# A seven-product block algorithm in the first layer of the second MLP, for the last 2048 of 3072 tokens

## The chip, the core and the metric

The kernel runs on one core of a Trainium2 chip. The metric is the device time of one execution in microseconds (us). TensorE multiplies matrices and writes its results to PSUM; VectorE and ScalarE do the elementwise work; GpSimd hardly takes part; SyncE issues the transfers between HBM and on-chip memory. In the rows of the profile PE is TensorE's multiplications, PEld its weight loads, DVE is VectorE, ACT is ScalarE, SPq is SyncE's queue.

## The reference

Chunked attention with a few memory keys gives 3072 tokens of 512 values; two MLPs follow, each 512 to 2048 to 512. The change touches the second one alone:

```python
def _moe2_ref(x, w_in, w_out, s, b):      # x (3072, 512), w_in (512, 2048), w_out (2048, 512)
    h = x @ w_in
    r = np.maximum(h, 0.0)
    g = s * (r * r) + b
    return (g @ w_out).astype(np.float32)
```

## The kernel before

All matrix products of the two MLPs are done in three multiplications instead of one: each operand is kept as a high and a low part whose sum is the fp32 value, and `mm3` (lines 289 to 293) adds high times high, high times low and low times high into the same PSUM tile. The three lines 291, 292 and 293 are the rows of every such product in the profile; the names on both sides of the arrow (`psH<-xh,w`, `acc<-w,gh`) tell first layer from second.

Tokens are taken in tiles of 384, eight per MLP, and the 2048 hidden values in sixteen chunks `c` of 128. One slot is one pair (tile, chunk). In a slot of the second MLP, `h2` (line 376) multiplies the four 128 by 128 blocks of the first weight with the token tile: 12 multiplications that each stream 384 token columns past loaded weights, into one of two `psH` tiles. Then the elementwise chain makes `g`: ReLU out of PSUM (line 379), square (380), scale and shift (382 or 384), high part (164), low part (168). `g` has one buffer, its two parts have three. Two slots later `out2` (line 387) uses the three blocks of 128 tokens of `g` as loaded weights and streams 512 columns of the second weight: 9 multiplications, into accumulators that fill the other half of PSUM over all sixteen chunks. `put_out` (line 327) copies a finished accumulator to SBUF, on ScalarE and VectorE in turn, into `big` tiles (four buffers), and SyncE writes them out.

The order on TensorE is that of the loop at line 551: first layer of slot n, second layer of slot n - 2, and so on without a gap. A scheduler then fills the other engines, so work whose inputs are there can be moved ahead of its place in the code. The weights of the second MLP arrive as integers of 64 bits and are unpacked on ScalarE and VectorE (`split_w`, lines 114 to 137), during the last tile of the first MLP and the first slots of the second. The tokens of a tile are loaded from HBM (`load_y`) and split into parts (`split_y`) while the tile before is computed. The first tile of an MLP is worked on in two halves of chunks, with the second tile between them.

```python
289      def mm3(o, a, b, sa, sb, first, last):
291          nc.tensor.matmul(o, sa(a[0]), sb(b[0]), start=first, stop=False)
292          nc.tensor.matmul(o, sa(a[0]), sb(b[1]), start=False, stop=False)
293          nc.tensor.matmul(o, sa(a[1]), sb(b[0]), start=False, stop=last)
```

Of the kernel before, what the change touches and what calls it, by code (L numbers as in the profile page):

```python
# [20 lines left out]
P = 128  # L21
# [28 lines left out]
def tile_attention_then_two_mlps(ctx, tc, q_in, k_in, v_in, w1, w2, s_in, b_in, out):  # L50
# [12 lines left out]

    nc = tc.nc
# [15 lines left out]
    N2 = 384  # L80
    NTILE2 = NT // N2

# [5 lines left out]
    gp = ctx.enter_context(tc.tile_pool(name="gp", bufs=3))  # L88
# [6 lines left out]
    part_dram = [dp.tile([P, KT, MAXN], F32, name="part1"), dp.tile([P, N2 // P, DM], F32, name="part2")]  # L95
# [10 lines left out]
    W = {}  # L106
# [7 lines left out]
    def split_w(c, i, raw):  # L114
# [21 lines left out]
        W[nm, c] = (hi, lo)  # L136
# [9 lines left out]
    op = [actx.enter_context(tc.tile_pool(name="op", bufs=4))]  # L146
# [116 lines left out]
    def to_x(u, ps, behind=None):  # L263
# [7 lines left out]
        for i in ins if behind else ():  # L271
            tc.add_manual_dep(i.ins, behind.ins.name,
                              mybir.DependencyInfo(mybir.DependencyClass.Sync, mybir.DependencyReason.DATA))
# [15 lines left out]
    def mm3(o, a, b, sa, sb, first, last):  # L289
# [3 lines left out]
        nc.tensor.matmul(o, sa(a[1]), sb(b[0]), start=False, stop=last)  # L293
# [10 lines left out]
    def split_g(g, n):  # L304
        gh = gp.tile([P, MAXN], F32R, tag="gh", name="gh")
        gl = gp.tile([P, MAXN], F32R, tag="gl", name="gl")
        hi_copy("gh", gh[:, :n], g[:, :n])
        sub(gl[:, :n], g[:, :n], gh[:, :n])
        return gh, gl
# [54 lines left out]

    def load_y(t):
        ys = p2["ys"].tile([P, KT, N2], F32, tag="ys", name="ys")
        nc.sync.dma_start(out=ys, in_=y_dram[:, :, t * N2:(t + 1) * N2])
# [3 lines left out]
    def split_y(t, m):  # L371
        ys, yh, yl = Y[t]
        hi_copy("yh", yh[:, m, :N2], ys[:, m, :])
        sub(yl[:, m, :N2], ys[:, m, :], yh[:, m, :N2])

    def h2(t, c):
        ps = h_mm(t, c, N2, Y[t][1:])
        g = one.tile([P, N2], F32, tag="g", name="g")
        nc.scalar.activation(out=g, in_=ps[:, :N2], func=AF.Relu)  # L379
# [5 lines left out]
        G[2, t, c] = split_g(g, N2)  # L385

    def out2(t, c):
        first, last = first_last(2, t, c)
        if first:
            accumulators(t, N2 // P)  # L390
        g = G.pop((2, t, c))
        for m in range(N2 // P):
            mm3(ACC[t][m], g, W["o", c], lambda a: a[:, m * P:(m + 1) * P], lambda a: a, first, last)
        put_out(2, t, c, DM, lambda m: out[t * N2 + m * P:t * N2 + (m + 1) * P, :])
# [87 lines left out]
    def mlp1_step(t, c):  # L482
# [41 lines left out]
    def mlp2_step(t, c):  # L524
# [91 lines left out]
```

## Time and profile before

| | us |
|---|---|
| median of 3 runs (1162.07 to 1163.25) | 1162.56 |
| the profiled execution's own time | 1160.43 |
| its span, first to last instruction | 1158.7 |
| TensorE multiplications busy, of the span | 1141.1 |
| TensorE weight loads busy | 1071.9 |
| VectorE busy | 688.4 |
| ScalarE busy | 455.2 |

The busy time of multiplications overlaps itself: each one's recorded duration reaches into the next one's, so the time of one in a stream is read from the distance between two starts. The same holds for weight loads. In rows grouped by line the columns are: line, engine, operation, output and inputs, shapes and count; then busy time in us and mean duration in ns; then the idle time before, with what ended it. In the rows in order of time, the first number is the start and the second the duration, both in us. In the rows by stretch, each engine has its busy time and in brackets its count of instructions; then come the granted clock of TensorE (1.00 is full), the share of the DMA engines and GB/s.

### The profile page before, as it was taken

The page shows a single profiled execution, that of the slowest core. Times are in us where ns is not written, and L with a number is a line of the kernel's source. Part 1 is how long each engine was busy: PE and PEld are TensorE (multiplying, and loading weights), DVE is VectorE, ACT ScalarE, POOL GpSimd, SP SyncE. Part 2 cuts the span into 40 slices and gives each one's busy share as a digit, 9 for nine tenths or more (in the row PEclk, how much of TensorE's full clock was granted, in tenths as well). Part 3 has the DMA queues.
Part 4 walks back from the last instruction along what each step waited for, and adds up shares of the span by engine and source line. Part 5 has one row for each costly group of instructions (what it writes and reads, how often), then busy time and mean ns, then how long its engine had stood idle before and what let it go on. Part 6 is the DMA issues. An engine that isn't in the chain of part 4 may idle for free.

```text
span 1158.7 us, 21163 instructions
## 1 busy us (share of the span) xinstructions
PE 1141.1 (98%) x8878; PEld 1071.9 (93%) x8878; DVE 688.4 (59%) x1430; ACT 455.2 (39%) x885; POOL 0.7 (0%) x6
## 2 busy tenths in 40 slices
PE   7989999999999999999999999999999999999998
PEld 6889999999999999999998999999999999999997
DVE  6999567776677766766799423343434344343433
ACT  4898432222222222222899544422323222232222
POOL 0000000000000000000000000000000000000000
PEclk7999999999999999999999999999999999999999
DMA  8963023112131121201874000210101000000000
GB/s 311 381 237 120 1 101 120 47 46 74 53 112 48 46 74 49 91 2 29 286 252 151 28 1 28 65 45 1 55 1 55 1 28 28 1 28 1 28 1 27
DMA packets 34271, 88.39 MB, mean 76 GB/s; under 512 B 3712, under 2 KB 12928, under 8 KB 34176
## 3 DMA queue, kind: packets, MB, share of 16 engines
q1 hardware_dynamic: 34176, 87.05, 21.6%
q8 instruction: 69, 1.13, 0.4%
q14 instruction: 26, 0.21, 0.1%
HBM read 72.88 MB, written 14.16 MB: 75 GB/s over the span
## 4 chain that ended last, share of the span: by engine, by line
PE 89%; ACT 6%; DVE 3%; issue 1%; DMA 0%; ACTq 0%
PE psH L291 14%; PE psH L293 14%; PE psH L292 14%; PE acc L292 14%; PE acc L293 14%; PE acc L291 14%; ACT raw L120 1%; PE psVS L259 1%; ACT w L134 1%; ACT raw L121 1%; PE psVS L200 1%; PE psV L259 1%; ACT g L315 1%; ACT g L316 1%; ACT gh L164 1%
## 5 line engine op out<-in xcount | busy, mean ns | idle before, releaser
L291 PE MATMUL psH<-xh,w 128*128 128x384 f32 x1024 | 346.7, 339 | 4.4 <-DVE g L317 2.4
L293 PE MATMUL psH<-xh,w 128*128 128x384 f32 x1024 | 344.7, 337 | 0.0
L292 PE MATMUL psH<-xl,w 128*128 128x384 f32 x1024 | 343.7, 336 | 0.2 <-DVE xl L168 0.2
L291 PEld LDWEIGHTS psH<-xh,w 128*128 128x128 f32 x1024 | 192.7, 188 | 13.9 <-DVE g L317 4.2
L380 DVE TENSOR_TENSOR g<-g 128x384 f32<-128x384 f32 x128 | 71.4, 558 | 219.4 <-ACT g L379 219.4
L292 PEld LDWEIGHTS psH<-xl,w 128*128 128x128 f32 x1024 | 192.7, 188 | 6.0 <-DVE xl L168 0.4
L168 DVE TENSOR_TENSOR gl<-g,gh 128x384 fp32r<-128x384 f32 x256 | 142.4, 556 | 91.3 <-ACT gh L164 88.7
L293 PEld LDWEIGHTS psH<-xh,w 128*128 128x128 f32 x1024 | 192.5, 188 | 0.2
L291 PE MATMUL acc<-gh,w 128*128 128x384 f32 x512 | 172.3, 337 | 0.0
L293 PE MATMUL acc<-gh,w 128*128 128x384 f32 x512 | 171.1, 334 | 0.0
L292 PE MATMUL acc<-gl,w 128*128 128x384 f32 x512 | 171.1, 334 | 0.0
L315 ACT ACTIVATE g<-psH 128x384 f32<-128x384 f32 x128 | 62.8, 491 | 272.8 <-PE psH L293 202.3
L379 ACT ACTIVATE g<-psH 128x384 f32<-128x384 f32 x128 | 63.1, 493 | 230.7 <-PE psH L293 227.4
L293 PE MATMUL acc<-w,gl 128*128 128x512 f32 x384 | 151.9, 396 | 0.0
L292 PE MATMUL acc<-w,gh 128*128 128x512 f32 x384 | 151.7, 395 | 0.0
L291 PE MATMUL acc<-w,gh 128*128 128x512 f32 x384 | 149.5, 389 | 1.4 <-DVE big L344 1.4
L164 ACT ACTIVATE gh<-g 128x384 fp32r<-128x384 f32 x176 | 92.5, 525 | 113.8 <-DVE g L384 99.1
L317 DVE SCALAR_TENSOR_TENSOR g<-g,psH 128x384 f32<-128x384 f32 x128 | 70.5, 551 | 99.5 <-ACT g L316 98.5
L291 PEld LDWEIGHTS acc<-gh,w 128*128 128x128 f32 x512 | 96.1, 188 | 0.8
L292 PEld LDWEIGHTS acc<-gl,w 128*128 128x128 f32 x512 | 96.1, 188 | 0.0
L293 PEld LDWEIGHTS acc<-gh,w 128*128 128x128 f32 x512 | 96.1, 188 | 0.0
L239 DVE STREAM_TRANSPOSE pt<-sm 32x128 f32<-32x128 f32 x288 | 87.2, 303 | 5.1
(62 smaller groups left out, 961.4 us busy)
## 6 DMA issues: line engine op xcount, KB each, us to landing
raw<-w SPq DMA_DIRECT2D x64, 512.0 KB, 5.1
kb<-k SPq DMA_DIRECT2D x24, 512.0 KB, 5.5
v<-v SPq DMA_DIRECT2D x24, 512.0 KB, 3.9
q<-q SPq DMA_DIRECT2D x24, 256.0 KB, 5.3
y_dram<-big SPq DMA_DIRECT2D x32, 192.0 KB, 1.9
ys<-y_dram SPq DMA_DIRECT2D x8, 768.0 KB, 4.9
out<-big SPq DMA_DIRECT2D x24, 256.0 KB, 2.1
part<-big SPq DMA_DIRECT2D x4, 192.0 KB, 3.3
```

The costliest lines, as they stand in the source:

```text
L120: nc.scalar.activation(out=f(high), in_=f(high), func=AF.Copy, scale=2.0 ** -112)
L164: return nc.scalar.activation(out=hi, in_=src, func=AF.Copy)
L168: return nc.vector.tensor_tensor(out=lo, in0=src, in1=f(hi), op=ALU.subtract)
L239: nc.vector.transpose(out=pt[k * CH:(k + 1) * CH, :, rows], in_=sm[rows, :, z, n0:n0 + CH])
L259: nc.tensor.matmul(ps[r % 2 * D:(r % 2 + 1) * D, z, o:o + CH], v[rows, (r * NC + c) * D:(r * NC + c + 1) * D], pt[rows, r, cs], start=True ...
L291: nc.tensor.matmul(o, sa(a[0]), sb(b[0]), start=first, stop=False)
L292: nc.tensor.matmul(o, sa(a[0]), sb(b[1]), start=False, stop=False)
L293: nc.tensor.matmul(o, sa(a[1]), sb(b[0]), start=False, stop=last)
L315: nc.scalar.activation(out=g[:, :n], in_=ps[:, :n], func=AF.Relu, scale=-1.0)
L317: nc.vector.scalar_tensor_tensor(out=g[:, :n], in0=g[:, :n], scalar=-1.0, in1=ps[:, :n], op0=ALU.add, op1=ALU.max)
L379: nc.scalar.activation(out=g, in_=ps[:, :N2], func=AF.Relu)
L380: nc.vector.tensor_tensor(out=g, in0=g, in1=g, op=ALU.mult)
```

## The change

Tiles of the second MLP become 384, 384 and 256 tokens, then four of 512. The first three are computed as before. For the tiles of 512, `h2` gives way to `h2_pair`, which handles two chunks at once. The first weight of two chunks is seen as two by two blocks (two halves of the 512 inputs, two chunks), the token tile as two by two blocks (two halves of the inputs, two halves of 256 tokens), and the four result blocks come from seven block products in place of eight, in Winograd's form of Strassen's algorithm. Each block product is two 128-deep steps in three parts, so six multiplications of 256 columns: 42 for a pair of chunks. The second layer of a pair is 24 multiplications of 512 columns.

The sums that go into the products are made elsewhere. Four sums of weight blocks per pair of chunks are made once (`make_s`), split into high and low parts, written to HBM, and read back for each pair of each tile (`load_s`) into places of the first weight that the products don't read. Four sums of token blocks are made per tile (`sums_y`, `split_blocks`). Seven additions per pair put the results together out of PSUM (`add` in `h2_pair`); they wait for the last multiplication into the PSUM bank that they read. The `g` chain then works on both chunks at once (`g2_pair`). The parts of `g` get four buffers in place of three, the `big` tiles three in place of four.

```diff
-    N2 = 384
-    NTILE2 = NT // N2
+    sizes2 = [384, 384, 256] + [512] * 4
+    assert sum(sizes2) == NT
+    starts2 = [sum(sizes2[:i]) for i in range(len(sizes2))]
+    NTILE2, NORM2 = len(sizes2), 3
...
-    gp = ctx.enter_context(tc.tile_pool(name="gp", bufs=3))
+    gp = ctx.enter_context(tc.tile_pool(name="gp", bufs=4))
...
+    s_dram = dp.tile([NF // 2, 4, P, 2, 2 * P], F32, name="s_dram")
...
-    op = [actx.enter_context(tc.tile_pool(name="op", bufs=4))]
+    op = [actx.enter_context(tc.tile_pool(name="op", bufs=3))]
...
+    HN = 256
+    def make_s(i):
+        a = []
+        for c in (2 * i, 2 * i + 1):
+            hi, lo = W["i", c]
+            t = wst.tile([P, DM], F32, tag="t", name="t")
+            nc.vector.tensor_tensor(out=t, in0=f(hi), in1=f(lo), op=ALU.add)
+            a.append(t)
+        (a11, a12), (a21, a22) = ((t[:, :2 * P], t[:, 2 * P:]) for t in a)
+        u = p2["ts"].tile([P, 4, 2 * P], F32, tag="ts", name="sf")
+        for j, (x, y, op) in enumerate(((a21, a22, ALU.add), (u[:, 0], a11, ALU.subtract),
+                                        (a11, a21, ALU.subtract), (a12, u[:, 1], ALU.subtract))):
+            nc.vector.tensor_tensor(out=u[:, j], in0=x, in1=y, op=op)
+            sp = p2["s"].tile([P, 2, 2 * P], F32R, tag="s", name="s")
+            nc.scalar.activation(out=sp[:, 0], in_=u[:, j], func=AF.Copy)
+            sub(sp[:, 1], u[:, j], sp[:, 0])
+            nc.sync.dma_start(out=s_dram[i, j], in_=f(sp))
+    SW, pairs = {}, [(t, i) for t in range(NORM2, NTILE2) for i in range(NF // 2)]
+    def load_s(n):
+        if n < len(pairs):
+            for j in range(4):
+                SW[n, j] = WT["i", 2 * ((4 * n + j) % 8) + 1][:, :, :2 * P]
+                nc.sync.dma_start(out=f(SW[n, j]), in_=s_dram[pairs[n][1], j])
+    def sums_y(t):
+        ys = load_tokens(t)
+        (b11, b12), (b21, b22) = ((ys[:, k:k + 2, :HN], ys[:, k:k + 2, HN:]) for k in (0, 2))
+        ts = p2["ts"].tile([P, 2, 2, HN], F32, tag="ts", name="ts")
+        t2, t3 = ts[:, 0], ts[:, 1]
+        for o, x, y in ((t3, b22, b12), (b12, b12, b11), (t2, b22, b12)):
+            nc.vector.tensor_tensor(out=o, in0=x, in1=y, op=ALU.subtract)
+        Y[t] = [b11, b21, t2, t3, b12, b22, t2], []
+    def split_blocks(t, j):
+        src, parts = Y[t]
+        if j < 6:
+            if j % 3 == 0:
+                p2["xt"] = [xp.tile([P, 3, 512], F32R, tag=f"{nm}{j // 3 ^ 1}", name=nm) for nm in ("xh", "xl")]
+        else:
+            p2["xt"] = [p2["ts"].tile([P, 1, 512], F32R, tag=f"{nm}2", name=nm) for nm in ("xh", "xl")]
+            nc.vector.tensor_tensor(out=src[6], in0=src[1], in1=src[2], op=ALU.subtract)
+        xh, xl = (x[:, j % 3, :].rearrange("p (k n) -> p k n", k=2) for x in p2["xt"])
+        hi_copy("yh", xh, src[j])
+        sub(xl, src[j], xh)
+        parts.append((xh, xl))
+    def h2_pair(n):
+        t, i = pairs[n]
+        blocks = Y[t][1]
+        wa, wb = W["i", 2 * i], W["i", 2 * i + 1]
+        lo_k, hi_k = (lambda w: tuple(x[:, :2 * P] for x in w)), (lambda w: tuple(x[:, 2 * P:] for x in w))
+        s1, s2, s3, s4 = ((SW[n, j][:, 0], SW[n, j][:, 1]) for j in range(4))
+        big = ps_a.tile([P, 2, 512], F32, tag="a", name="psG")
+        hs = [ps_h.tile([P, 512], F32, tag="h", name="psG") for _ in range(2)]
+        place = [big[:, 0, :HN], big[:, 0, HN:2 * HN], big[:, 1, :HN], big[:, 1, HN:2 * HN],
+                 hs[0][:, :HN], hs[0][:, HN:2 * HN], hs[1][:, :HN]]
+        last = []
+        for o, a, b in zip(place, (lo_k(wa), hi_k(wa), s2, s3, s1, s4, hi_k(wb)), blocks):
+            for k in range(2):
+                mm = mm3(o, a, b, lambda x: x[:, k * P:(k + 1) * P], lambda x: x[:, k, :], k == 0, k == 1)
+            last.append(mm)
+        q1, q2, q6, q7, q5, q3, q4 = place
+        hb = p2["ts"].tile([P, 2, 512], F32, tag="hb", name="hb")
+        m1, u2, u3 = (wst.tile([P, DM], F32, tag="t", name=nm)[:, :HN] for nm in ("m1", "u2", "u3"))
+        def add(o, x, q, behind):
+            wait(nc.vector.tensor_tensor(out=o, in0=x, in1=q, op=ALU.add), last[behind])
+        wait(nc.scalar.activation(out=m1, in_=q1, func=AF.Copy), last[1])
+        add(hb[:, 0, :HN], m1, q2, 1)
+        add(u2, m1, q6, 3)
+        add(u3, u2, q7, 3)
+        add(u2, u2, q5, 5)
+        add(hb[:, 1, HN:], u3, q5, 5)
+        add(hb[:, 0, HN:], u2, q3, 5)
+        add(hb[:, 1, :HN], u3, q4, 6)
+        return hb
+    def g2_pair(t, i, hb):
+        nc.vector.scalar_tensor_tensor(out=hb, in0=hb, scalar=0.0, in1=hb, op0=ALU.max, op1=ALU.mult)
+        nc.scalar.activation(out=hb, in_=hb, func=AF.Identity, scale=s_sb, bias=b_sb)
+        for z in range(2):
+            G[2, t, 2 * i + z] = split_g(hb[:, z], 512)
...
-            op.append(ctx.enter_context(tc.tile_pool(name="op2", bufs=4)))
-            p2["ys"] = ctx.enter_context(tc.tile_pool(name="ysp", bufs=1))
+            op.append(ctx.enter_context(tc.tile_pool(name="op2", bufs=3)))
+            p2["ys"] = p2["ts"] = ctx.enter_context(tc.tile_pool(name="ysp", bufs=1))
+            p2["s"] = ctx.enter_context(tc.tile_pool(name="sp", bufs=2))
...
+        if hf + 4 <= n < hf + 4 + NF and n % 2 == 0:
+            make_s((n - hf - 4) // 2)
+        if t == 2 and c in (8, 9, 10):
+            split_blocks(NORM2, c - 8)
+        if t == 2 and c == 10:
+            load_s(0)
...
+    load_s(1)
+    for j in range(3, 7):
+        split_blocks(NORM2, j)
+    behind = [(NORM2 - 1, NF - 2), (NORM2 - 1, NF - 1)]
+    for n_, (t, i) in enumerate(pairs):
+        hb = h2_pair(n_)
+        load_s(n_ + 2)
+        if i == 3 and t + 1 < NTILE2:
+            sums_y(t + 1)
+        if i == NF // 2 - 1 and t + 1 < NTILE2:
+            for j in range(7):
+                split_blocks(t + 1, j)
+        g2_pair(t, i, hb)
+        for slot in behind:
+            out2(*slot)
+        behind = [(t, 2 * i), (t, 2 * i + 1)]
+    for slot in behind:
+        out2(*slot)```

The first order that matters is TensorE's. In the code before, a slot's 12 first-layer rows of 384 columns are followed by 9 second-layer rows of 512; here the last rows of such a slot's first layer (`w0` is the first weight, `w1` the second) and the first of the second layer:

```order
L291 MATMUL psH_10318<-xh_9625,w0_10_7668 128x384
L292 MATMUL psH_10318<-xl_9626,w0_10_7668 128x384
L293 MATMUL psH_10318<-xh_9625,w0_10_7668 128x384
L291 MATMUL acc0_10085<-w1_8_7552,gh_10271 128x512
L292 MATMUL acc0_10085<-w1_8_7552,gh_10271 128x512
L293 MATMUL acc0_10085<-w1_8_7552,gl_10272 128x512
```

After the change, the seventh product of a pair and the first rows of the second layer of the pair before (`psG` are the PSUM tiles of the products; `mm3` stands at lines 302 to 304 there):

```order
L302 MATMUL psG_9362<-xh_9169,w0_5_7245 128x256
L303 MATMUL psG_9362<-xl_9170,w0_5_7245 128x256
L304 MATMUL psG_9362<-xh_9169,w0_5_7245 128x256
L302 MATMUL psG_9362<-xh_9169,w0_5_7245 128x256
L303 MATMUL psG_9362<-xl_9170,w0_5_7245 128x256
L304 MATMUL psG_9362<-xh_9169,w0_5_7245 128x256
L302 MATMUL acc0_9334<-w1_2_7020,gh_9326 128x512
L303 MATMUL acc0_9334<-w1_2_7020,gh_9326 128x512
L304 MATMUL acc0_9334<-w1_2_7020,gl_9327 128x512
```

Rows of 256 columns stand where rows of 384 stood, 42 in a row for a pair, and 24 rows of the second layer follow; nothing else is on TensorE between them.

The second is VectorE's in the tiles of 512. Before, two slots of a late tile give:

```order
L380 TENSOR_TENSOR g_10738<-g_10738 128x384
L384 TENSOR_SCALAR g_10738<-g_10738,s_sb_90,b_sb_91 128x384
L168 TENSOR_TENSOR gl_10743<-g_10738,gh_10742 128x384
L380 TENSOR_TENSOR g_10770<-g_10770 128x384
L384 TENSOR_SCALAR g_10770<-g_10770,s_sb_90,b_sb_91 128x384
L168 TENSOR_TENSOR gl_10775<-g_10770,gh_10774 128x384
```

After, one pair of chunks gives:

```order
L478 TENSOR_TENSOR hb_9696<-m1_9697,psG_9651 128x256
L478 TENSOR_TENSOR u2_9698<-m1_9697,psG_9651 128x256
L478 TENSOR_TENSOR u3_9699<-u2_9698,psG_9651 128x256
L478 TENSOR_TENSOR u2_9698<-u2_9698,psG_9652 128x256
L478 TENSOR_TENSOR hb_9696<-u3_9699,psG_9652 128x256
L478 TENSOR_TENSOR hb_9696<-u2_9698,psG_9652 128x256
L478 TENSOR_TENSOR hb_9696<-u3_9699,psG_9653 128x256
L491 SCALAR_TENSOR_TENSOR hb_9696<-hb_9696 128x1024
L175 TENSOR_TENSOR gl_9715<-hb_9696,gh_9714 128x512
L175 TENSOR_TENSOR gl_9719<-hb_9696,gh_9718 128x512
```

Seven additions out of PSUM, one square of 1024 columns and two low parts stand where six operations of 384 columns stood; scale and shift are on ScalarE alone.

The third is VectorE's at the start of the second MLP, where the last weights are unpacked (`t`, `raw`, `w0_13`) between the `g` operations of the first slots. Before:

```order
L380 TENSOR_TENSOR g_7408<-g_7408 128x384
L128 SCALAR_TENSOR_TENSOR t_7895<-raw0_13_7244,t_7895 128x512
L125 SCALAR_TENSOR_TENSOR t_7933<-raw1_13_7246 128x512
L168 TENSOR_TENSOR w1_12_7869<-t_7857,w1_12_7869 128x512
L128 SCALAR_TENSOR_TENSOR t_7933<-raw1_13_7246,t_7933 128x512
L168 TENSOR_TENSOR gl_7413<-g_7408,gh_7412 128x384
```

After, from the low part of the same slot to that of the next:

```order
L175 TENSOR_TENSOR gl_7417<-g_7412,gh_7416 128x384
L175 TENSOR_TENSOR s_7844<-sf_7842,s_7844 128x256
L420 TENSOR_TENSOR sf_7842<-sf_7842,t_7838 128x256
L398 TENSOR_TENSOR g_7454<-g_7454 128x384
L420 TENSOR_TENSOR sf_7842<-t_7838,sf_7842 128x256
L175 TENSOR_TENSOR s_7849<-sf_7842,s_7849 128x256
L132 SCALAR_TENSOR_TENSOR t_7886<-raw1_12_7205 128x512
L132 SCALAR_TENSOR_TENSOR t_7924<-raw0_13_7248 128x512
L175 TENSOR_TENSOR gl_7459<-g_7454,gh_7458 128x384
```

The sums of `make_s` (`sf`, `s`) are scheduled from the third slot on, mixed with the rest of the unpacking, and the unpacking of the last chunks is spread over more slots.

## Rows read from the trace of the kernel before

**Rows 1.** The page: busy time by engine; granted clock in 40 slices.

```profile
PE 1141.1 (98%) x8878; PEld 1071.9 (93%) x8878; DVE 688.4 (59%) x1430; ACT 455.2 (39%) x885; POOL 0.7 (0%) x6
PEclk7999999999999999999999999999999999999999
```

**Rows 2.** What TensorE waited for in the second MLP: us, times, longest.

```profile
PE acc L291 <- DVE big L344: 1.4, 1, 1.4
```

**Rows 3.** TensorE in order of time, one slot of the second MLP.

```profile
901.07 0.39 PE L291 MATMUL acc<-w,gh 128*128 128x512 f32 x1
...
902.92 0.39 PE L293 MATMUL acc<-w,gl 128*128 128x512 f32 x1
903.15 0.33 PE L291 MATMUL psH<-xh,w 128*128 128x384 f32 x1
...
905.09 0.33 PE L293 MATMUL psH<-xh,w 128*128 128x384 f32 x1
905.26 0.39 PE L291 MATMUL acc<-w,gh 128*128 128x512 f32 x1
```

**Rows 4.** The ReLU of line 379, one per slot: first and last start.

```profile
L379 ACT ACTIVATE g<-psH x108: 492/492/492, 700.3 to 1148.3; 128x384 f32<-128x384 f32 x108
```

**Rows 5.** Multiplications in order of time after attention's, in the first MLP.

```profile
269.74 0.44 PE L291 MATMUL psH<-xh,w 128*128 128x384 f32 x1
270.02 0.34 PE L292 MATMUL psH<-xl,w 128*128 128x384 f32 x1
...
270.89 0.33 PE L291 MATMUL psH<-xh,w 128*128 128x384 f32 x1
```

**Rows 6.** The weight loads of the same stretch, in order of time.

```profile
269.73 0.19 PEld L291 LDWEIGHTS psH<-xh,w 128*128 128x128 f32 x1
269.84 0.19 PEld L292 LDWEIGHTS psH<-xl,w 128*128 128x128 f32 x1
270.02 0.19 PEld L293 LDWEIGHTS psH<-xh,w 128*128 128x128 f32 x1
```

**Rows 7.** By stretch: a stretch with much DMA traffic, in the first MLP.

```profile
600.00:608.00 8.00, 8.00 (x47) 7.74 (x45) 7.97 (x15) 8.00 (x17) 0.00 (x0) 1.00 0.75 242
```

**Rows 8.** VectorE and ScalarE by line and shape, 700 to 1157 us.

```profile
L380 DVE TENSOR_TENSOR g<-g 128x384 f32<-128x384 f32 x108 | 60.3, 558 | 199.2 <-ACT g L379 199.2
...
L164 ACT ACTIVATE gh<-g 128x384 fp32r<-128x384 f32 x108 | 56.6, 524 | 99.4 <-DVE g L384 99.1
...
L382 ACT ACTIVATE g<-g,b_sb,s_sb 128x384 f32<-128x384 f32 x12 | 8.5, 706 | 6.3 <-DVE g L380 6.3
L346 ACT ACTIVATE big<-acc 128x512 f32<-128x512 f32 x14 | 8.3, 593 | 7.9 <-PE acc L293 7.8
L344 DVE COPY big<-acc 128x512 f32<-128x512 f32 x7 | 4.8, 691 | 6.7 <-ACT big L346 6.7
```

**Rows 9.** VectorE's low part of `g`, in order of time, in Rows 3's slot.

```profile
903.46 0.56 DVE L168 TENSOR_TENSOR gl<-g,gh 128x384 fp32r<-128x384 f32 x1 [0.59 <-ACT gh L164]
```

**Rows 10.** By stretch: six stretches of 16 us, 624 to 720, and their sum.

```profile
624.00:640.00 16.00, 15.50 (x76) 13.71 (x77) 15.86 (x29) 13.52 (x26) 0.00 (x0) 1.00 0.26 82
640.00:656.00 16.00, 16.00 (x82) 14.47 (x81) 7.87 (x14) 9.01 (x17) 0.00 (x0) 1.00 0.00 1
...
sum 96.00, PE 95.50 PEld 86.24 DVE 43.46 ACT 51.32 POOL 0.00; mean PE 15.92 PEld 14.37 DVE 7.24 ACT 8.55 POOL 0.00
```

**Rows 11.** The end of the span, in order of time, all engines.

```profile
1153.77 1.28 ACT L346 ACTIVATE big<-acc 128x512 f32<-128x512 f32 x2 [3.33 <-PE acc L293]
...
1154.02 0.39 PE L293 MATMUL acc<-w,gl 128*128 128x512 f32 x1
...
1154.40 0.69 DVE L344 COPY big<-acc 128x512 f32<-128x512 f32 x1 [3.37 <-ACT big L346]
```

**Rows 12.** The page's DMA issues: size and median us to landing.

```profile
out<-big SPq DMA_DIRECT2D x24, 256.0 KB, 2.1
```

More of the change, by code (lines that the diff above doesn't have):

```diff
@@ L135, in split_w @@
         sub(lo, f(t), hi)
-        W[nm, c] = (hi, lo)
+        W[nm, c], WT[nm, c] = (hi, lo), parts
         yield
@@ L292, in mm3 @@
         nc.tensor.matmul(o, sa(a[0]), sb(b[1]), start=False, stop=False)
-        nc.tensor.matmul(o, sa(a[1]), sb(b[0]), start=False, stop=last)
+        return nc.tensor.matmul(o, sa(a[1]), sb(b[0]), start=False, stop=last)
     G, ACC = {}, {}
@@ L372, in split_y @@
         ys, yh, yl = Y[t]
-        hi_copy("yh", yh[:, m, :N2], ys[:, m, :])
-        sub(yl[:, m, :N2], ys[:, m, :], yh[:, m, :N2])
+        n = sizes2[t]
+        hi_copy("yh", yh[:, m, :n], ys[:, m, :])
+        sub(yl[:, m, :n], ys[:, m, :], yh[:, m, :n])
     def h2(t, c):
-        ps = h_mm(t, c, N2, Y[t][1:])
-        g = one.tile([P, N2], F32, tag="g", name="g")
-        nc.scalar.activation(out=g, in_=ps[:, :N2], func=AF.Relu)
+        n = sizes2[t]
+        ps = h_mm(t, c, n, Y[t][1:])
+        g = one.tile([P, MAXN], F32, tag="g", name="g")[:, :n]
+        nc.scalar.activation(out=g, in_=ps[:, :n], func=AF.Relu)
         nc.vector.tensor_tensor(out=g, in0=g, in1=g, op=ALU.mult)
@@ L389, in out2 @@
         if first:
-            accumulators(t, N2 // P)
+            accumulators(t, sizes2[t] // P)
         g = G.pop((2, t, c))
-        for m in range(N2 // P):
+        for m in range(sizes2[t] // P):
             mm3(ACC[t][m], g, W["o", c], lambda a: a[:, m * P:(m + 1) * P], lambda a: a, first, last)
-        put_out(2, t, c, DM, lambda m: out[t * N2 + m * P:t * N2 + (m + 1) * P, :])
+        put_out(2, t, c, DM, lambda m: out[starts2[t] + m * P:starts2[t] + (m + 1) * P, :])
     def attn_steps():
@@ L540, in mlp2_step @@
             weights_to(w2, 52 + 4 * n, 0)
-        if nxt < NTILE2 and c0 + 2 <= c < c0 + 2 + KT:
-            split_y(nxt, c - c0 - 2)
+        if first and 2 <= c < 2 + KT:
+            split_y(1, c - 2)
+        if t == 0 and hf + 2 <= c < hf + 2 + KT:
+            split_y(2, c - hf - 2)
+        if hf + 4 <= n < hf + 4 + NF and n % 2 == 0:
[4 more added lines that the diff above has]
+            load_s(0)
         yield
@@ L548, in tile_attention_then_two_mlps @@
         order = [(0, c) for c in range(HF[mlp])] + [(1, c) for c in range(NF)] + [(0, c) for c in range(HF[mlp], NF)]
-        order += [(t, c) for t in range(2, NTILE1 if mlp == 1 else NTILE2) for c in range(NF)]
+        order += [(t, c) for t in range(2, NTILE1 if mlp == 1 else NORM2) for c in range(NF)]
         seq += [(step, out_mm, t, c) for t, c in order]
-    for n_ in range(len(seq) + 2):
-        if n_ < len(seq):
-            step, _, t, c = seq[n_]
-            parts = step(t, c)
-            next(parts)
+    for n_, (step, _, t, c) in enumerate(seq):
+        parts = step(t, c)
+        next(parts)
         if n_ >= 2:
@@ L558, in tile_attention_then_two_mlps @@
             out_mm(t, c)
-        if n_ < len(seq):
-            next(parts)
+        next(parts)
+    load_s(1)
[15 more added lines that the diff above has]
+    for slot in behind:
+        out2(*slot)
 def pack(q, k, v, mem_k, mem_v):
```

38 lines of the change are left out of this document (24 added, 14 removed).

## The prediction

> **What bounds the kernel now.** I read the page first: multiplications fill 98% of the span at full granted clock from the second slice on, VectorE 59%, ScalarE 39% [rows 1]. Then the waits of the second MLP alone: TensorE waited there for anything but itself once, 1.4 us in some 535 [rows 2]. So this stage lasts as long as its stream of multiplications, and the change is priced by how many there are and how far apart they start. One slot in order of time gives both distances: nine second-layer multiplications of 512 columns from 901.07 to 903.15, so 0.231 us each, and twelve first-layer ones of 384 from 903.15 to 905.26, so 0.176 each [rows 3]. The ReLU, one per slot, confirms the period over 107 slots: (1148.3 - 700.3) / 107 = 4.187 us [rows 4].
>
> **What goes and what comes on TensorE.** The 2304 tokens behind the first two tiles were six tiles of 384, 96 slots: 96 x 4.187 = 401.9 us go. What comes: the second layer's columns stay the same in number, 32 pairs x 24 + 16 slots x 6 = 864 multiplications of 512, at 0.231: 199.6 us. The first layer becomes 32 x 42 = 1344 multiplications of 256 columns for the products and 16 x 12 = 192 of 256 for the tile of 256 tokens: 1536 x c. Everything hangs on c, the distance between two starts at 256 columns, which the trace does not show for this kind of product. The change is even at c = (401.9 - 199.6) / 1536 = 0.1317 us, and each nanosecond is 1.54 us of time. Seven products for eight save an eighth of the columns, but a distance that shrank less than the columns would give it back.
>
> **The value of c.** Shrinking with the columns would give 0.176 x 256 / 384 = 0.117. A line through this stage's two sizes, 0.176 at 384 and 0.231 at 512, gives 0.1205. In the first MLP 384 columns take (270.89 - 270.02) / 5 = 0.174 [rows 5], and the line from there to 0.231 gives 0.117. The other limit is the weight load that each multiplication has. Its recorded 0.19 us is longer than any of these values, but it is not its distance: where TensorE comes from attention's small products, two loads start at 269.73 and 269.84, so a load occupies its path for 0.11 us, and the next waits for the multiplication [rows 6]. The first multiplication there, whose load is not hidden, is followed 0.28 us later, the second 0.17 us later [rows 5]: 0.28 = 0.11 + 0.17, a load shown and a load hidden. So the low end is 0.111 (a load and its start), the high end 0.174, no gain below 384 columns, if loads hid less well than I read. I take 0.120, the line of the same stage: gain 1536 x (0.1317 - 0.120) = 18.0 us. Loads and multiplications would then be nearly equal, 0.11 against 0.12, still with the multiplication ahead.
>
> The Trainium skill, "TensorE: Matmul & The Clock Gate", section "Back-to-back issue gap", gives N / 2.4 + 2.5 ns for a single multiplication's gap, so 109 ns at 256 columns; by it the sum would be an estimated 1536 x 0.0225 = 35 us of gain. The same formula gives 162 and 216 ns where rows 3 show 176 and 231, so the measurement decides and I keep 0.120.
>
> **Work on the other engines.** Prices of 256 and 1024 columns come from 558 ns at 384 and 691 at 512 on VectorE [rows 8]: about 0.43 and 1.22 us. In the tiles of 512 a pair lasts 24 x 0.231 + 42 x 0.12 = 10.6 us on TensorE. VectorE has 7 x 0.43 + 1.22 + 2 x 0.69 = 5.6 us per pair, and per tile some 13 more operations of 512 columns (sums, low parts, copies), 1.1 us per pair: 63%. ScalarE has less: a copy, scale and shift of 1024 columns (between 0.71 and, scaled from 384 columns, 1.9 us) and two high parts of 0.6. The chain behind the last product is 0.43 + 1.22 + 1.9 + 0.6 + 0.7 = 4.9 us to the first chunk's parts, 5.6 to the second's; they are needed after the second layer of the pair before (5.5) and the next pair's products (5.0), so 5 us are to spare. PSUM is free half a microsecond after the last product and wanted 5.5 us after it. At a tile's end seven splits of 0.69 stand on VectorE before the square, which takes most of that spare time and none of TensorE's.
>
> Each pair reads 1 MB of sums back, about 100 GB/s, with a pair's time to land; SyncE is in order, so a read that waits for its place holds up the token load and the outputs behind it, which have 5 us or more too. Traffic does not slow the stream: at 242 GB/s, 47 multiplications of 384 columns started in 8 us, 0.170 each [rows 7].
>
> The weight sums cost VectorE 2 x 0.69 + 8 x 0.43 = 4.8 us for a pair of chunks, 38 us in all. From 624 to 720 us VectorE is busy 43.5 of 96 us, so 52 are free; but the first 16 us are full, 15.9 [rows 10], and the order puts the sums right there. What they displace is the unpacking of late chunks, which nobody waits for yet. The `g` chain may slip: a low part ended at 904.02 [rows 9] and its first reader on TensorE starts two slots after the 901.07 one's followers, at 901.07 + 2 x 4.19 = 909.45, so 5.4 us to spare. In the order, the longest stretch between two low parts is 11 operations, about 6.5 us for a slot of 4.19. Between 0 (all hidden) and 8 us (the sums that the order puts into the first 32 us, 3.5 x 4.8 = 16.8, less the 8.3 that are free there by rows 10); I take 1, with the two tile transitions, since the slip of one slot is inside the spare time. Adding work excludes a gain.
>
> The end: today the last multiplication starts at 1154.02 and VectorE's last copy at 1154.40 [rows 11]. With four copies per tile and three `big` buffers, the fourth waits for the first one's output to land. The first copy can start when its pair of accumulators is done, six multiplications (1.4 us) before the stream's end; it takes 0.59 and lands 2.1 us later [rows 8, 12], 1.3 us after the end, and the fourth then takes 0.69: it ends near 2.0, where 0.7 was; 1.3 us. In the first MLP the same wait falls inside the 3 us before that accumulator is written again; 0, at worst 0.5 at each of its eight tiles.
>
> **The sum.** 18.0 - 1.0 - 1.3 = 15.7 us. The profiled execution takes 1160.43, so it would take 1144.7; the median of the runs lies 2.1 above it, so 1162.56 - 15.7 = 1146.9, rounded 1147. About 0.2% (2.3 us) is what a measurement of this kernel can tell from no change.
>
> **The rivals.** First, c near the load's own distance, 0.111 to 0.116 [rows 6]: 24 to 32 us of gain, 1133 to 1140. For it: lines from the first MLP bend that way; against: both sizes seen here lie 0.015 above their columns' pace. Second, the other side: weight loads become the bound. The mechanism is the hand-over of the loaded weights: at 384 columns a load of 0.19 has 0.17 to overlap with; if two loads cannot follow each other faster than the load's recorded time less the 0.015 by which they overlap now, c is 0.174, and the cost is 1536 x 0.042 = 65 us, 1228; halfway, 0.145, it is 20 us, 1185. It decides from 0.1317 on. For it: no full-width fp32 product of this short length is in the stage; against: the 0.11 between two starts. Third, the slipping chain: VectorE's sums in the busy first slots, or a read of sums that holds SyncE's queue, take 5 to 12 us, 1152 to 1160; it decides where a slip passes 5.4 us. Fourth, c between 0.126 and 0.131, because load and multiplication disturb each other when nearly equal: 1155 to 1165, about no change. That the products are not done as said I exclude by the order: 42 rows of 256 columns, then 24 of 512.
>
> The first rows that TensorE runs after attention show hidden loads at 0.17. The Trainium skill, same page, section "The mechanism" of its part on packing small matmuls, says that a load overlaps a running multiplication only where their row groups differ. By that rule every product would show its load, 0.11 + 0.12, and the time would be 1162.56 + 1536 x 0.098 = 1313 us; the steady 0.17 behind the first 0.28 [rows 5] speaks against it, and I give it 1 in 100, within the slower cases.
>
> **How the numbers follow.** Forecast (c 0.116 to 0.125, small waits), 1140 to 1155: 0.60. The low rival: 0.13. The slipping chain: 0.10. About even, 1160 to 1165: 0.06. Weight loads the bound: 0.11. Faster is then 0.60 + 0.13 + 0.09 = 0.82, the same 0.05, slower 0.13. The range from 1136 to 1163 leaves out half of the low rival and the slow cases, 2 in 10.
>
> **What would show it.** In the changed profile, 42 starts of 256 columns should span 5.0 us and 24 of 512 columns 5.5; loads should start 0.12 apart, right behind the multiplications' starts. A wait of TensorE on `gl`, `hb` or `w0` rows means the third rival, products 0.14 or more apart with loads back to back the second. The last copy should wait for a transfer. I am wrong if a pair takes over 11.2 us, which is what its 512 tokens take today (2.67 slots x 4.187).

## The result, and the profile after

The changed kernel takes 1149.91 us (median of 4 runs, 1149.35 to 1150.90) where the kernel before, run beside it, takes 1162.32 (1161.11 to 1163.25): a ratio of 0.9895, interval 0.9878 to 0.9912, 12.4 us less. The forecast was 15.7 us less, 1147, with a range of 1136 to 1163. Its sign held and the time lies in the range. But one term of the sum is off by some 7 us, twice as much as the whole, and another by 2.6 us the other way.

The profiled execution took 1149.35 us, its span 1147.6; that of before was 1160.43. The page, as in [rows 1]:

```profile
PE 1124.5 (98%) x9262; PEld 1057.3 (92%) x9262; DVE 767.9 (67%) x1617; ACT 475.0 (41%) x890; POOL 0.7 (0%) x6
PEclk7999999999999999999999999999999999999999
```

TensorE still fills 98% of a span that is 11.1 us shorter, with more multiplications. One pair of chunks on TensorE in order of time (start, duration, instruction), which answers to [rows 3]:

```profile
905.93 0.28 PE L302 MATMUL psG<-xh,w 128*128 128x256 f32 x1
...
910.84 0.28 PE L304 MATMUL psG<-xh,w 128*128 128x256 f32 x1
910.96 0.40 PE L302 MATMUL acc<-w,gh 128*128 128x512 f32 x1
...
912.12 0.39 PE L304 MATMUL acc<-w,gl 128*128 128x512 f32 x1
...
916.43 0.28 PE L302 MATMUL psG<-xh,w 128*128 128x256 f32 x1
```

The 42 multiplications of the seven products take 910.96 - 905.93 = 5.03 us, 0.120 each, and the 24 of the second layer 916.43 - 910.96 = 5.47: a pair in 10.50 us. That the period holds can be seen in the copy that opens each pair's additions, ScalarE's on line 480 (count, duration min/median/max, first and last start):

```profile
L480 ACT ACTIVATE m<-psG x32: 363/383/384, 806.7 to 1129.5; 128x256 f32<-128x256 f32 x32
```

(1129.5 - 806.7) / 31 = 10.41, since the first of the 31 distances holds only 12 second-layer multiplications and is 2.7 us shorter; the other 30 are 10.50. VectorE's operations by shape, the counterparts of [rows 8] (busy us and mean ns; idle before):

```profile
L491 DVE SCALAR_TENSOR_TENSOR hb<-hb 128x1024 f32<-128x1024 f32 x32 | 39.2, 1225 | 0.9
L478 DVE TENSOR_TENSOR hb<-u,psG 128x256 f32<-128x256 f32 x96 | 34.5, 416 | 0.0
```

TensorE's waits between 100 and 640 us (in all, times, longest; [rows 2] has one of 1.4 us for the second MLP, and before 600 us the kernel before has none):

```profile
PE acc L302 <- DVE big L355: 5.2, 4, 2.3
PE acc L302 <- DVE big L351: 1.5, 1, 1.5
```

From 640 us to the end the same view is empty: TensorE waits for no `gl`, `hb` or `w0`. So the second MLP goes as the forecast says, and something new happens ahead of it. Between the first second-layer multiplication of the second MLP and the last of all lie 632.23 to 1142.14 = 509.9 us, where 624.50 to 1154.02 = 529.5 lay before: 19.6 us less. The first of these starts, however, comes 7.7 us later, and behind the last one the span has 5.4 us in place of 4.6. The ledger of the two profiled executions is -19.6 + 7.7 + 0.8 = -11.1 us.

### The profile page after: what moved, and what is told of

Its sections match the earlier page's. It is cut to its first block, busy times and chain, and to the rows that moved or that the text cites. A ratio compares the mean times of both kernels' runs of the same rounds, so it can differ in the third digit from the quotient of the medians.

```text
span 1147.6 us, 22472 instructions
## 1 busy us (share of the span) xinstructions
PE 1124.5 (98%) x9262; PEld 1057.3 (92%) x9262; DVE 767.9 (67%) x1617; ACT 475.0 (41%) x890; POOL 0.7 (0%) x6
## 4 chain that ended last, share of the span: by engine, by line
PE 87%; DVE 5%; ACT 5%; DMA 2%; issue 1%; SPq 0%; DVEq 0%; ACTq 0%
PE acc L302 14%; PE acc L303 14%; PE acc L304 14%; PE psH L302 9%; PE psH L304 9%; PE psH L303 9%; PE psG L304 5%; PE psG L303 5%; PE psG L302 5%; PE psVS L266 1%; DVE pt L246 1%; PE psVS L207 1%; ACT raw L127 1%; DMA raw<-w 1%; ACT w L141 1%
## 5 line engine op out<-in xcount | busy, mean ns | idle before, releaser
L302 PE MATMUL psH<-xh,w 128*128 128x384 f32 (+1 forms) x704 | 235.4, 334 | 3.7 <-DVE g L328 2.0
L304 PE MATMUL psH<-xh,w 128*128 128x384 f32 (+1 forms) x704 | 233.8, 332 | 0.0
L303 PE MATMUL psH<-xl,w 128*128 128x384 f32 (+1 forms) x704 | 233.4, 332 | 0.2 <-DVE xl L175 0.2
L326 ACT ACTIVATE g<-psH 128x384 f32<-128x384 f32 x128 | 63.0, 492 | 278.9 <-PE psH L304 207.0
L302 PE MATMUL acc<-gh,w 128*128 128x384 f32 x512 | 173.2, 338 | 4.7 <-DVE big L355 3.2
L304 PE MATMUL acc<-gh,w 128*128 128x384 f32 x512 | 172.2, 336 | 0.0
L303 PE MATMUL acc<-gl,w 128*128 128x384 f32 x512 | 172.2, 336 | 0.0
L302 PE MATMUL acc<-w,gh 128*128 128x512 f32 x384 | 150.4, 392 | 2.0 <-DVE big L355 2.0
L303 PE MATMUL acc<-w,gh 128*128 128x512 f32 x384 | 150.6, 392 | 0.0
L304 PE MATMUL acc<-w,gl 128*128 128x512 f32 x384 | 150.1, 391 | 0.0
L302 PEld LDWEIGHTS psH<-xh,w 128*128 128x128 f32 x704 | 133.0, 189 | 8.5 <-DVE g L328 2.7
L303 PEld LDWEIGHTS psH<-xl,w 128*128 128x128 f32 x704 | 133.0, 189 | 2.4 <-DVE xl L175 0.4
L304 PEld LDWEIGHTS psH<-xh,w 128*128 128x128 f32 x704 | 133.0, 189 | 0.2
L304 PE MATMUL psG<-xh,w 128*128 128x256 f32 x448 | 126.9, 283 | 0.0
L303 PE MATMUL psG<-xl,w 128*128 128x256 f32 x448 | 126.9, 283 | 0.0
L302 PE MATMUL psG<-xh,w 128*128 128x256 f32 x448 | 126.7, 283 | 0.0
L175 DVE TENSOR_TENSOR gl<-g,gh 128x384 fp32r<-128x384 f32 (+1 forms) x176 | 95.8, 544 | 29.7 <-ACT gh L171 27.1
L302 PEld LDWEIGHTS acc<-gh,w 128*128 128x128 f32 x512 | 96.5, 189 | 6.2 <-DVE big L355 3.8
L304 PEld LDWEIGHTS acc<-gh,w 128*128 128x128 f32 x512 | 96.7, 189 | 0.0
L303 PEld LDWEIGHTS acc<-gl,w 128*128 128x128 f32 x512 | 96.7, 189 | 0.1
## 6 DMA issues: line engine op xcount, KB each, us to landing
raw<-w SPq DMA_DIRECT2D x64, 512.0 KB, 4.7
w<-s_dram SPq DMA_DIRECT2D x128, 256.0 KB, 3.6
kb<-k SPq DMA_DIRECT2D x24, 512.0 KB, 5.5
v<-v SPq DMA_DIRECT2D x24, 512.0 KB, 3.9
s_dram<-s SPq DMA_DIRECT2D x32, 256.0 KB, 2.0
q<-q SPq DMA_DIRECT2D x24, 256.0 KB, 5.4
y_dram<-big SPq DMA_DIRECT2D x32, 192.0 KB, 1.9
out<-big SPq DMA_DIRECT2D x24, 256.0 KB, 2.1
```

The costliest lines, as they stand in the source:

```text
L175: return nc.vector.tensor_tensor(out=lo, in0=src, in1=f(hi), op=ALU.subtract)
L304: return nc.tensor.matmul(o, sa(a[1]), sb(b[0]), start=False, stop=last)
L326: nc.scalar.activation(out=g[:, :n], in_=ps[:, :n], func=AF.Relu, scale=-1.0)
```

## Where the 7.7 us went

The same first-layer multiplication of the first MLP starts 0.9 us later than before at 100 us, 2.0 at 150, 4.1 at 200, and stays about there until 563 us, where 4 us come at once. The last three places are ends of tiles or of a half tile, where accumulators are copied into `big` tiles. The 0.9 us at 100 are not: 1.4 us are there at 35 us, before the first copy into a `big` tile at 73 us, and other profiled executions with three buffers, such as that of the doubled reads below, have nothing of it at 100 us. They are a difference between executions. At 563 us, VectorE's copies and TensorE in order of time (in brackets the idle time before and what ended it):

```profile
558.72 0.56 DVE L355 COPY big<-acc 128x384 f32<-128x384 f32 x1 [0.78 <-ACT big L357]
...
563.33 0.34 PE L302 MATMUL acc<-gh,w 128*128 128x384 f32 x1
565.39 0.56 DVE L355 COPY big<-acc 128x384 f32<-128x384 f32 x1 [1.71 <-DMA y_dram<-big]
566.00 0.44 PE L302 MATMUL acc<-gh,w 128*128 128x384 f32 x1 [2.34 <-DVE big L355]
...
566.88 0.52 PE L303 MATMUL acc<-gl,w 128*128 128x384 f32 x1
567.20 0.52 PE L304 MATMUL acc<-gh,w 128*128 128x384 f32 x1
...
570.08 0.37 PE L302 MATMUL acc<-gh,w 128*128 128x384 f32 x1
```

Three copies (two of them ScalarE's) are done by 559.5; the fourth has no buffer until the first output has landed, at 565.4, and TensorE needs the accumulator that it empties. The wait has a tail: behind it ten distances of 0.32 us stand (566.88 to 570.08), nearly twice the usual 0.17, 1.5 us more in all. By stretch (length, busy time and count of each engine, granted clock, DMA share, GB/s) the clock is at the lower of its two levels there, 1.2 in place of 2.4 GHz, after TensorE stood nearly idle from 563 to 566:

```profile
563.00:566.00 3.00, 0.67 (x4) 0.35 (x2) 1.29 (x4) 0.52 (x1) 0.00 (x0) 1.00 0.87 337
566.88:569.76 2.88, 2.88 (x11) 2.88 (x10) 1.11 (x2) 2.36 (x5) 0.00 (x0) 0.50 0.93 277
```
Why the output took so long is in the DMA issues from 558 to 567 us (count, KB each, median us to landing):

```profile
raw<-w SPq DMA_DIRECT2D x2, 512.0 KB, 5.7
ys<-y_dram SPq DMA_DIRECT2D x1, 768.0 KB, 6.8
y_dram<-big SPq DMA_DIRECT2D x4, 192.0 KB, 6.5
```

The first three of the four outputs stand behind a token load of 768 KB and weights of 512 KB and land after some 6.5 us; the median of all 32 on the page of the profile is 1.9. The Trainium skill, "SBUF — State Buffer", section "The DMA setup-cost knee", fits a transfer's time in us as 2 + bytes / 436,000, by which 192 KB would take an estimated 2.45. The measured median of 1.9 is near that, the 6.5 behind other transfers far from it. In the kernel before, the outputs at this place were late too, with nobody waiting for them (its issues from 552 to 562 us):

```profile
y_dram<-big SPq DMA_DIRECT2D x4, 192.0 KB, 5.4
```

At 198 us it is another chain. Token tile 0 is done in two halves, and the first half's four parts are read back into `big` tiles before the sums are formed there; with three, the fourth part is fetched only when a sum has left:

```profile
193.84 1.48 DVE L351 TENSOR_TENSOR big<-big,acc 128x384 f32<-128x384 f32 x3
194.42 1.29 SPq L358 DMA_DIRECT2D y_dram<-big  x3
196.33 0.32 SPq L345 DMA_DIRECT2D big<-part  x1
198.82 0.55 DVE L351 TENSOR_TENSOR big<-big,acc 128x384 f32<-128x384 f32 x1
199.42 0.45 PE L302 MATMUL acc<-gh,w 128*128 128x384 f32 x1 [1.50 <-DVE big L351]
```

Out, landed, in, landed: 4.4 us between the end of the first sum (194.4) and the fourth's start, more than the accumulator can wait. At 150 us, the end of tile 1, TensorE waits 0.8 us for the fourth copy. There the outputs land in 1.9 us, and the copy stands behind three of attention's transposes in VectorE's order; in the kernel before it stood ahead of them.

## The experiments

My theory: products at 0.120 are the gain, and the three `big` buffers cost what lies ahead of the second MLP. The rivals: the late start comes with the new second MLP (weight sums, transitions, reads), or the weight loads limit the products, so that a part of the gain is lost there.

**Three buffers in the kernel before.** The edit, in the kernel before, and nothing else:

```
-    op = [actx.enter_context(tc.tile_pool(name="op", bufs=4))]
+    op = [actx.enter_context(tc.tile_pool(name="op", bufs=3))]
```

> The kernel before with three big buffers in place of four up to the end of the first MLP, nothing else. Theory (the loss in the first MLP is the fourth copy of an accumulator, which waits for the first one's output to land): TensorE waits on big at ends of tiles of the first MLP, the second MLP begins some 7 to 8 us later than in the kernel before, about 1170 us. Rival (the loss comes from another part of the change, such as the order or the wider parts of g): no change, 1162 to 1163.

Measured: 1165.60 us against 1161.90, ratio 1.0031 (1.0021 to 1.0040): 3.7 us, half of what I expected. The waits at 150 and 198 us are there, with the 4 to 5 us by 250 us; the jump at 563 is not. The kernel opens a second pool, `op2`, when the last tile of the first MLP begins, and that still had four; the outputs at 563 us, of the tile before, are already copied into it.

**Both pools.** The same edit, and `bufs=4` to 3 for `op2` also.

> The kernel before with three big buffers in place of four in both pools, the one of the tiles of the first MLP and the one that takes over in its last tile. Theory, that the late start of the second MLP in the changed kernel is all due to the number of big buffers: the pool of the tiles alone gave 1165.6 with 4.5 to 5 us lost by 250 us and no jump at 563 us; with the second pool cut too the jump at about 563 us must come back, 3 to 5 us with its multiplications at the lower clock behind it, so 1169 to 1170, and the second MLP's first output multiplication starts about 8 us later than in the kernel before. Rival, that the jump belongs to the change of the second MLP itself (its transitions or its prepared sums): no jump, about 1166.

Measured: 1168.99 (1168.09 to 1170.36) against 1161.72, ratio 1.0060 (1.0043 to 1.0077): 7.3 us. TensorE's waits between 100 and 645 us:

```profile
PE acc L291 <- DVE big L344: 6.5, 4, 2.8
PE acc L291 <- DVE big L340: 1.7, 1, 1.7
```

They stand at the places of the changed kernel's, under the old line numbers, with 1.5 us more in sum, and the second MLP's first output multiplication starts at 632.11, 7.6 us later than before. No part of the new second MLP is in this kernel, so its weight sums and transitions are not needed for the late start. Each start is that of one execution: in the other runs of the changed kernel with three buffers in both pools it lies between 630.2 and 633.8 us.

**Four buffers in the changed kernel.** `op` from 3 to 4; to have room, the parts of `g` get three buffers instead of four.

```
-    gp = ctx.enter_context(tc.tile_pool(name="gp", bufs=4))
+    gp = ctx.enter_context(tc.tile_pool(name="gp", bufs=3))
-    op = [actx.enter_context(tc.tile_pool(name="op", bufs=3))]
+    op = [actx.enter_context(tc.tile_pool(name="op", bufs=4))]
```

> The changed kernel with four big buffers up to the end of the first MLP; to make room the parts of g have three buffers, not four. Theory (buffer): the second MLP begins at 623 us as in the kernel before, about 1142.5 us. Rival (loss from elsewhere): 1150. Should three buffers for g hold the pairs up, TensorE waits on gl or gh after 800 us, and a pair lasts over 10.4 us.

Measured: 1146.09 (1145.20 to 1148.54), ratio 0.9862 (0.9845 to 0.9879), 3.8 us better than the changed kernel and not the 7.4 expected, for the same reason: `op2` still had three. The waits at 150 and 198 us are gone, those from 563 us on are not. The products stay at 0.120 with three `g` buffers.

**Four in both pools.** The edit above and `op2` from 3 to 4.

> As the run with four big buffers, and four of them in the second MLP too. Theory (the last copy waits for a transfer at the end): 1.3 us less than that run, about 1141; the last copy follows the third without a wait. Rival: the end is set by the transfers themselves, no change.

Measured: 1141.49 (1140.57 to 1143.27), ratio 0.9821 (0.9807 to 0.9836). It is the fastest kernel here, 20.4 us below the kernel before and 8.4 below the change. That the expected 1141 was met is luck: from the run with four buffers in one pool it was to be 1.3 us and is 4.6, because `op2` also serves the last two ends of the first MLP, and that run had been expected 3.6 us too low. TensorE's waits between 100 and 645 us are again the single one of [rows 2], and from 552 to 562 us the outputs land as late as in the changed kernel, with nobody waiting for them:

```profile
PE acc L302 <- DVE big L355: 1.4, 1, 1.4
```

```profile
y_dram<-big SPq DMA_DIRECT2D x4, 192.0 KB, 7.0
```

The first output multiplication of the second MLP starts at 625.93 here, so 6.3 of the 7.7 us are gone. The 1.4 that are left stand beside no wait that the kernel before doesn't have.

The end of the span also shows what a fourth buffer is worth there. The last copies, of the changed kernel and of this one, in order of time:

```profile
1142.14 0.39 PE L304 MATMUL acc<-w,gl 128*128 128x512 f32 x1
1143.95 0.69 DVE L355 COPY big<-acc 128x512 f32<-128x512 f32 x1 [1.42 <-DMA out<-big]
```

```profile
1134.92 0.39 PE L304 MATMUL acc<-w,gl 128*128 128x512 f32 x1
1135.97 0.69 DVE L355 COPY big<-acc 128x512 f32<-128x512 f32 x1 [0.67 <-ACT big L357]
```

1.81 us behind the last multiplication with three, 1.05 with four: the tail's wait for a landed output is real and costs 0.8.

**Eight products, 512 columns.** The changed kernel with the first layer of its four tiles of 512 done plainly: no sums, no reads, no additions, 24 multiplications of 512 columns for a pair where seven products had 42 of 256.

```
-        for o, a, b in zip(place, (lo_k(wa), hi_k(wa), s2, s3, s1, s4, hi_k(wb)), blocks):
-            for k in range(2):
...
+        for z in range(2):
+            ps = ps_h.tile([P, 512], F32, tag="h", name="psG")
+            for k, xx in enumerate(Y[t][1]):
+                mm3(ps, W["i", 2 * i + z], xx, lambda a: a[:, k * P:(k + 1) * P], lambda a: a, k == 0, k == KT - 1)
```

> The changed kernel with the plain first layer in the tiles of 512: 24 multiplications of 512 columns per pair of chunks, no sums of weights or tokens, no reads of sums; the second layer is as in the changed kernel. Theory (TensorE's stream bounds the stage, and what the other engines do for the seven products is hidden): a pair takes 24 x 0.228 = 5.47 in place of 42 x 0.12 = 5.04 us, so 32 x 0.43 = 14 us more, about 1164. Rival (sums, additions and reads cost TensorE time in the changed kernel): the difference is smaller, 1150 to 1158.

Measured: 1159.61 (1156.89 to 1162.02), ratio 0.9977 (0.9967 to 0.9988), 9.7 us above the change. The stretch of the second MLP is 521.9 us, 12.0 more than with seven products. So of its 19.6 us, 12.0 are the seven products, and 7.6 come with the wider tiles. The medians differ by less than the stretch; in the profiled execution of this run the second MLP also starts 2.0 us earlier than in the changed kernel's. I had expected 14 for the stretch; here is why it is less. One pair of this kernel on TensorE:

```profile
902.12 0.39 PE L302 MATMUL acc<-w,gh 128*128 128x512 f32 x1
...
907.56 0.39 PE L302 MATMUL psG<-xh,w 128*128 128x512 f32 x1
...
913.00 0.39 PE L302 MATMUL acc<-w,gh 128*128 128x512 f32 x1
```

48 multiplications in 10.88 us are 0.2267 each, not the 0.231 of [rows 3]. In a stream of one width the distance is shorter. In the changed kernel's pair above, the first five behind the change of width take (912.12 - 910.96) / 5 = 0.232 and the nineteen others (916.43 - 912.12) / 19 = 0.2268. In the kernel before every run of 512 columns but one is nine long, and all nine average 0.231. The one is its last, 27 in a row up to the 1154.02 of [rows 11]:

```profile
1148.09 0.39 PE L291 MATMUL acc<-w,gh 128*128 128x512 f32 x1
...
1150.17 0.39 PE L291 MATMUL acc<-w,gh 128*128 128x512 f32 x1
```

The first nine distances take (1150.17 - 1148.09) / 9 = 0.231 there and the seventeen behind them (1154.02 - 1150.17) / 17 = 0.2265, so the shorter distance could be read before the change.

**Eight products, 256 columns.** As the last one, but in blocks of 256: 48 multiplications of 256 columns for a pair in place of 42.

> As the run with the plain first layer in tiles of 512, but each product in blocks of 256 columns: 48 multiplications of 256 per pair of chunks in place of 24 of 512. Theory (0.12 us per multiplication of 256 columns, whoever uses it, and TensorE's stream bounds the stage): 48 x 0.12 = 5.75 us per pair, 0.3 more than with 24 of 512 (5.44) and 0.72 more than with 42: some 10 us above that run, 23 above the changed kernel, about 1170 to 1173. Rival (the changed kernel's stage is bound by something besides the stream): less than 15 us above the changed kernel.

Measured: 1171.89 (1170.88 to 1172.94), ratio 1.0079 (1.0064 to 1.0094), 22.0 above the change. 32 x 6 x 0.12 = 23.0 was to come. At equal block size the eighth product costs what its multiplications say; the plain layer gets part of that back by streaming 512 columns.

**No weight sums.** `make_s` writes raw parts of the weights to where the sums belong and computes nothing, so the products are of other numbers.

```
-            nc.vector.tensor_tensor(out=u[:, j], in0=x, in1=y, op=op)
...
+            nc.sync.dma_start(out=s_dram[i, j], in_=f(WT["i", 2 * i + j // 2][:, :, j % 2 * 2 * P:(j % 2 + 1) * 2 * P]))
```

> The changed kernel without the sums of weight blocks: parts of the weights themselves are written in their place, so VectorE and ScalarE do none of that work and the products are of other numbers. Theory (the sums are hidden): 1149 to 1150, no change beyond 1 us. Rival (they hold up the g chain at the start of the second MLP, my third rival): 5 to 8 us less, 1142 to 1145.

Measured: 1149.62 (1146.78 to 1153.12), ratio 0.9886 (0.9858 to 0.9915); the difference to the change, 0.3 us, is below what can be told. By stretch of 16 us from 624 to 720 us, the sums of the changed kernel and of this one, as in [rows 10]:

```profile
sum 96.00, PE 94.00 PEld 84.91 DVE 78.81 ACT 64.30 POOL 0.00; mean PE 15.67 PEld 14.15 DVE 13.13 ACT 10.72 POOL 0.00
```

```profile
sum 96.00, PE 93.44 PEld 84.57 DVE 49.84 ACT 54.59 POOL 0.00; mean PE 15.57 PEld 14.10 DVE 8.31 ACT 9.10 POOL 0.00
```

29 us of VectorE's work vanish and TensorE is no busier. The stretch of the second MLP, 633.76 to 1143.50, is 509.7 us long, against 509.9 with the sums. The sums are hidden.

**Reads twice.** Each read of weight sums is issued twice, 2 MB per pair.

```
-                nc.sync.dma_start(out=f(SW[n, j]), in_=s_dram[pairs[n][1], j])
+                for _ in range(2):
+                    nc.sync.dma_start(out=f(SW[n, j]), in_=s_dram[pairs[n][1], j])
```

> The changed kernel with every read of weight sums done twice, so 2 MB per pair. Theory (reads are hidden and traffic does not slow the stream): 1150, products still 0.12 apart. Rival (the queue of SyncE or the traffic counts): TensorE waits on w0 tiles, over 1155.

Measured: 1148.75 (1146.65 to 1150.21), ratio 0.9879 (0.9862 to 0.9896), the same as the change. The products stay at 0.120, and TensorE waits for none of the reads; the one new wait is 0.8 us for a `big` tile at 667 us. Reads of sums have room for as much again.

**Halved products.** Each product multiplication is cut into two of 128 columns: 84 for a pair, the same columns, twice the weight loads.

```
-            for k in range(2):
-                mm = mm3(o, a, b, lambda x: x[:, k * P:(k + 1) * P], lambda x: x[:, k, :], k == 0, k == 1)
+            for m in range(2):
+                for k in range(2):
+                    mm = mm3(o[:, m * P:(m + 1) * P], a, b, lambda x: x[:, k * P:(k + 1) * P],
+                             lambda x: x[:, k, m * P:(m + 1) * P], k == 0, k == 1)
```

> The changed kernel with every multiplication of the seven products cut into two of 128 columns: 84 per pair in place of 42, each with its weight load. It asks how near 256 columns are to the point where the loads set the distance. Theory (a load occupies 0.11 us, so two multiplications cannot start closer than 0.111): 84 x 0.111 = 9.3 us per pair in place of 5.0, 32 x 4.3 = 137 us more, about 1287, and the first rival of the prediction's price for loads stands. Rival (the distance keeps shrinking with the columns, as from 512 to 384 to 256, to 0.065 at 128): 84 x 0.065 = 5.5 us, 14 us more, 1164.

Measured in a single execution: 1291.66 us, 142 above the change, near the 137 of the theory and far from the 14 of its rival. Multiplications and loads in order of time:

```profile
999.84 0.19 PEld L303 LDWEIGHTS psG<-xl,w 128*128 128x128 f32 x1
999.90 0.28 PE L303 MATMUL psG<-xl,w 128*128 128x128 f32 x1
999.95 0.19 PEld L304 LDWEIGHTS psG<-xh,w 128*128 128x128 f32 x1
1000.01 0.28 PE L304 MATMUL psG<-xh,w 128*128 128x128 f32 x1
1000.06 0.19 PEld L302 LDWEIGHTS psG<-xh,w 128*128 128x128 f32 x1
1000.12 0.28 PE L302 MATMUL psG<-xh,w 128*128 128x128 f32 x1
```

Half the columns start 0.111 us apart, not 0.06, with loads every 0.11 that overlap the multiplication before. The bound is thus 0.111, and 256 columns at 0.120 are just above it. That the load sets it, and not the multiplication, is argued: it equals the 0.11 between the two loads of [rows 6]; no run here changes the loads alone. The Trainium skill, "TensorE: Matmul & The Clock Gate", section "LDWEIGHTS (loading the stationary operand)", gives P / 1.2 ns for the P columns of a load, 107 ns for 128. The 0.111 agrees within 4%; the recorded 0.19 is not the load's share of the path.

## Why the forecast was right, and where not

**The distance c** was forecast at 0.120 from a line through 384 and 512 columns, and came out at 0.1198 over 1344 multiplications. Its low end, 0.111, read from two loads after attention, is the bound that the halved products show. The second rival, loads that cannot follow each other so fast, is refuted by them, and so is the prediction's 1313 us, for loads that would not overlap at all. The 47 multiplications in 8 us, read from [rows 7] as 0.170 each, include two that had started before; 45 start there, 0.173 apart, which bears out the same point, that the traffic does not slow them. The pair was to take 10.6 us and takes 10.50.

**The stage** was to gain 18.0 - 1.0 = 17.0 us and gained 19.6. The step that failed is "the second layer's columns stay the same in number ... 864 multiplications of 512, at 0.231". With 24 in a row instead of nine, they average 5.47 / 24 = 0.228; over the 768 in tiles of 512, (0.2312 - 0.2279) x 768 = 2.5 us. I took the distance as a property of the width, and rows 3 held one run length only. Two smaller things cancel: the 1.0 us set aside for the other engines was hardly needed, and a wait of 0.9 us for a `big` tile at 634.8 us falls inside the stretch. With four buffers in both pools the stretch is 1134.92 - 625.93 = 509.0 us, a gain of 20.5.

**The other engines** cost nothing that the runs can tell: the sums' share of the 1 us is within the noise of the run without them. The square of 1024 columns was estimated at 1.22 us and takes 1.225, the additions at 0.43 and take 0.42. The third rival, a slipping chain, is absent from the waits.

**The tail** was to cost 1.3 us by a fourth copy that waits for a landed output; it does, and costs 0.8.

**The first MLP** is the step that failed and decided the size: "the same wait falls inside the 3 us before that accumulator is written again; 0, at worst 0.5 at each of its eight tiles". The second MLP starts 7.7 us later in the profile, of which four buffers take back 6.3, and another 0.9 inside the stretch; in the runs of the kernel before, three buffers in both pools cost 7.3. Three things were wrong in it. The landing time was a median of the whole profile, 2.1 us, where the outputs at 563 us had 6.5 behind weights and tokens. The parts of tile 0, which are read back into the same buffers, were not counted among their users, though `put_out` allots all four. And only waits were priced, where the clock's lower level behind the wait of 2.3 us took 1.5 more. The waits stand at four places only: the end of tile 1, the second half of tile 0, and the ends of the last two tiles, of which the last has one in the kernel before too. The other tiles' ends pay nothing, as forecast.

The ledger: 15.7 forecast, + 2.6 for the stage, + 0.5 for the tail, - 7.7 for the first MLP gives 11.1, the difference of the profiled executions. That the sum came as near as it did is in part luck: with the first MLP's error alone 8.0 would have been left.

Open: why a change of width lengthens the next five to nine distances; the traces show the pattern in every kernel here, not its cause.

## What to carry to other kernels

A smaller number of buffers has to be priced at each of its users, with the landing time that transfers have at that moment, not with the median over the whole profile; the DMA issues of the few microseconds around the end of the last tile but one, in the trace of the kernel before, show 5.4 us in place of the median's 1.9. When a change pays for room with a buffer elsewhere, try paying with another one: here three `g` buffers and four `big` buffers in both pools gained 8.4 us together, of which the `big` buffers explain 7.3 + 0.8, so there is no sign that the fourth `g` buffer was worth anything. And an eighth of the plain first layer would be 768 x 0.2267 / 8 = 21.8 us, of which seven products brought 12.0: at 0.1198, a multiplication of 256 columns takes 0.0064 us more than half of one of 512, 1344 x 0.0064 = 8.7 us. Most of the rest goes to the change of width, which the plain layer doesn't have: 32 x 5 x 0.005 = 0.8 us.

## What the runs showed of the hardware

The distance of two multiplications depends on what ran before them: at 512 columns 0.2267 us in a stream of one width, 0.232 for the first five after 256 columns, 0.231 for nine after 384. From 256 to 128 columns the distance falls only from 0.120 to 0.111. And one wait of 2.3 us was followed by 2.9 us at a granted clock of 0.50, the lower level, while the row of granted clock on the profile's page, in slices of 29 us, shows 9 (90% or more) in every slice but the first.
